# Who begins the wide weight loads and the rows of sums in an attention and feed-forward kernel: ScalarE's queue in place of SyncE's

## The chip, the cores and the metric

The kernel runs as one program on one core of a Trainium2 chip. A core has TensorE (PE), which multiplies matrices; VectorE (DVE), ScalarE (ACT) and GpSimd (POOL), which work element by element; SyncE (SP), which in this kernel only begins transfers; and 16 DMA engines that carry them out. The measure is the device time of one execution in microseconds (us); smaller is better.

## The reference, cut to what matters

```python
# attention: 4 batches, 8 heads, 576 rows, head size 64, causal by blocks of 64
scores = (1 / sqrt(D)) * q @ k.T
scores = where(block_i >= block_j, scores, -1e9)
attn = exp(scores - max(scores)); attn = attn / (sum(attn) + 1e-09)
x = (attn @ v) as [2304, 512]
# first feed-forward, 512 -> 1536 -> 512
xn = x / sqrt(mean(x * x) + 1e-06) * rms_g
g = xn @ w_gate;  x = (g * sigmoid(g) * (xn @ w_val)) @ w_out
# second feed-forward: 8 experts of 512 -> 1024 -> 512, weighted by P
P = exp(x @ gate - max), 8 times scaled by row sums and column sums
out = sum over e of P[:, e] * (relu(x @ w1[e]) @ w2[e])
```

All of it is in float32. A float32 operand is split into a high and a low part, and three fast products stand for one exact one.

## The kernel before, in words

**The planner.** The whole program is written down as a graph of operations. `G.op(engine, planned ns, function, r=, w=, prio=, lat=)` adds one: `r` and `w` are the buffers that it reads and writes, `lat` the planned time from its end to the start of what needs it, and `alts` other engines that may do it. `Graph.emit` then runs a list schedule forward and backward 24 times with these planned numbers, keeps the best, and writes the instructions out in that order. Each engine runs its own instructions strictly in that order. So a changed number or engine of one operation can move others, on every engine.

**The stages.** Attention takes the 32 heads one after another, four batches of eight. Heads 0 to 6 and 8 to 12 ("new" heads) make their scores twice: once for the maximum, once transposed for the exponent (L584, L587 on TensorE, L593 on ScalarE); their output and their sums of exponents come from one product (L620). The others normalise and transpose (L522, L683, L693, L733). The first feed-forward (L1007 up, L1066 down) works on five blocks of rows; its block 0 needs the first batch's attention, and it is laid between the heads of the next batches. The second feed-forward fills the rest.

**Rows of sums.** In `sv_d`, for each of the 12 new heads, the output of L620 is copied from PSUM to the buffer `tm` in two pieces, 512 and 64 wide (by ScalarE at L645, or by VectorE at L647, as the planner finds it better). Then a transfer of 2.2 KB spreads row 0, the sums, over 64 partitions (L653, begun by SyncE), VectorE adds 1e-9 and inverts (L657, L658), two more transfers write the result to DRAM and spread it over 64 partitions (L663, L664), and VectorE multiplies (L666, into `xx`).

**Wide loads.** The weights of the first feed-forward come as 64-bit words, 512 KB for a tile of 128 x 512. `convert` loads one into one of two buffers (L348, begun by SyncE; there are 36, 12 each of the matrices `wg`, `wv` and `wo`), ScalarE makes two integer parts (L350, L352), VectorE shifts (L354), GpSimd adds (L356, into `raw`). From `raw` come the high part (ACT, L294) and the low part (POOL or DVE, L307) of `w`, which SyncE stores for later blocks (L334) and reloads (L324). A wide load may begin when L350 and L352 of the load two before it are done.

**SyncE's queue** holds everything else too: q, k and v (L456, L457, L493, L494, L500), 1,093 transfers in all. It runs in order: a transfer that waits holds up those behind it. Eight semaphores are taken in turn by all transfers of the program, so a transfer also waits until the one that had its semaphore before has landed.

Of the kernel before, what the change touches and what calls it, by code (L numbers as in the profile page):

```python
# [12 lines left out]
U64 = mybir.dt.uint64  # L13
AF = mybir.ActivationFunctionType
# [183 lines left out]
def t_act(n, psum=False, ap=0):  # L198
    if ALONE:
        return (165 if psum else 190) + 0.845 * n + 144 * ap  # L200
    return (50 if psum else 92) + n / 1.2 + 90 * ap
# [9 lines left out]
def t_vv(n):  # L211
    return Both(150 + 1.04 * n if ALONE else t_v1(n))


def t_v1(n):
    return 150 + 1.04 * n if ALONE else 66 + n / 0.96


def t_v2(n):
    return Both(150 + n / 1.92 if ALONE else 120 + n / 0.96)  # L220


def t_pool(n):
    return Both(60 + 2.4 * n if ALONE else 60 + 2.28 * n)
# [11 lines left out]
def tile_attn_moe_moe2(ctx: ExitStack, tc: tile.TileContext, qT, kT, vP, wg, wv, wo, rg, gw, w1, w2, ident_d, mq_d, mk_d, bm_d, out):  # L236
    nc = tc.nc
# [11 lines left out]
    G = Graph()  # L249
# [10 lines left out]
    def fixed(t, par=False):  # L260
        return Buf(lambda: t, par=par)
# [50 lines left out]
    class Loader:  # L312
# [24 lines left out]
        def convert(self, src, raw, prio):  # L337

            wd, y, up = WIDE.next(), CVT[0].next(), CVT[1].next()

            def part(dt, i):
                return wd().bitcast(dt).rearrange("p (n w) -> p n w", w=2)[:, :, i]

            def i32(b):
                return b().bitcast(I32)

            ops = [
                G.op("SP", 2200, lambda: nc.sync.dma_start(out=wd().bitcast(U64), in_=src), w=[wd], prio=prio, lat=2000),  # L348

                G.op("ACT", t_act(512), lambda: nc.scalar.activation(out=y(), in_=part(F32, 1), func=AF.Prelu, scale=2.0**-112, alpha=2.0**32),  # L350
                     r=[wd], w=[y], prio=prio),
                G.op("ACT", t_act(512), lambda: nc.scalar.activation(out=i32(up), in_=part(U32, 0), func=AF.Copy, scale=2.0**-29),  # L352
                     r=[wd], w=[up], prio=prio),
                G.op("DVE", t_v2(512), lambda: nc.vector.tensor_scalar(  # L354
                    out=i32(y), in0=i32(y), scalar1=3, scalar2=None, op0=ALU.logical_shift_left), r=[y], w=[y], prio=prio),
                G.op("POOL", t_pool(512), lambda: nc.gpsimd.tensor_tensor(out=i32(raw), in0=i32(y), in1=i32(up), op=ALU.add),  # L356
                     r=[y, up], w=[raw], prio=prio),
            ]
            self.conv += ops
# [44 lines left out]
    def A(*a, **k):  # L404
        k.setdefault("prio", 1.0)
        o = G.op(*a, **k)
        att_ops.append(o)
        return o
# [209 lines left out]
    def sv(i, dst, d0, t, o, n, c, start, stop):  # L618
        p, vx = st["P", i][t], st["vs", i]
        A("PE", t_f32(n), lambda: nc.tensor.matmul(  # L620
            out=dst()[:, d0 : d0 + n], lhsT=vx()[:, c, :], rhs=p()[:, o : o + n], start=start, stop=stop),
            r=[vx, vones, p], w=[dst], prio=0.0)
# [13 lines left out]
    def sv_d(i):  # L636
        b, h = divmod(i, H)
        O, O2, r = st.pop(("O", i)), st.pop(("O2", i)), TM.next(par=True)
        sv(i, O2, 128, 0, 0, 64, 0, True, True)
        if h % 2 == 0:  # L640
            st["X", b, h // 2] = XX.next(par=True)
        X, p = st["X", b, h // 2], 64 * (h % 2)
        halves = ((O, 0, 64, 512), (O2, 128, 0, 64))
        for src, o, c, n in halves:
            A("ACT", t_act(n, True), lambda src=src, o=o, c=c, n=n: nc.scalar.activation(  # L645
                out=r()[:, c : c + n], in_=src()[:, o : o + n], func=AF.Copy), r=[src], w=[r],
              alts=[("DVE", t_v1(n), lambda src=src, o=o, c=c, n=n: nc.vector.tensor_copy(  # L647
                  out=r()[:, c : c + n], in_=src()[:, o : o + n]))], margin=0.0)
        sr, rc, rb, rd = SR.next(), RC.next(), (RB0 if i < H else RB1).next(), fixed(scr.tile([S], F32, name=f"rd{i}"))
        rt = lambda: O2()[0:64, 256 : 256 + S // 64]  # L650
        if i >= H:
            rb.before |= b0_ops
        A("SP", 600, lambda: nc.sync.dma_start(out=sr(), in_=r()[0:1, :].rearrange("o (p n) -> o p n", p=64)),  # L653
          r=[r], w=[sr], lat=2000, prio=0.5)

        def recip():
            nc.vector.tensor_scalar(out=rt(), in0=sr(), scalar1=1e-9, scalar2=None, op0=ALU.add)  # L657
            nc.vector.reciprocal(out=rc(), in_=rt())  # L658

        tmp = Buf(rt)  # L660
        tmp.before, tmp.users = O2.before, O2.users
        A("DVE", 380, recip, r=[sr], w=[rc, tmp], prio=0.5)
        A("SP", 600, lambda: nc.sync.dma_start(out=rd().rearrange("(p n) -> p n", p=64), in_=rc()), r=[rc], w=[rd], lat=2000, prio=0.5)  # L663
        A("SP", 600, lambda: nc.sync.dma_start(out=rb()[64:128], in_=rd().unsqueeze(0).to_broadcast([64, S])),  # L664
          r=[rd], w=[rb], lat=2000, prio=0.5)
        A("DVE", t_vv(S), lambda: nc.vector.tensor_tensor(  # L666
            out=X()[p : p + 64], in0=r()[64:128], in1=rb()[64:128], op=ALU.mult), r=[r, rb], w=[X])
# [261 lines left out]
    def attention():  # L929
# [8 lines left out]

        old = ((t_x0, nothing), (t_x1, pv_a), (t_x2, pv_b), (t_x3, pv_c), (nothing, pv_d))
        new = ((st_a, nothing), (st_b, sv_a), (st_c, sv_b), (st_d, sv_c), (nothing, sv_d))  # L940
        for i in range(NH + 1):
            p = i - 1
# [806 lines left out]
```

## Time and profile before

| | |
|---|---|
| time, median of 3 runs | 2167.6 us (2166.83 to 2169.93) |
| profiled execution, span from its first to its last instruction | 2165.9 us (no time of its own is listed beside it; the span is 1.7 us under the median) |
| busy share of the span | PE 99%, DVE 64%, POOL 53%, ACT 44% |
| granted TensorE clock, mean | 0.996 of full speed |
| DMA, mean | 194 GB/s |

Busy shares are means over stages that differ. TensorE's own share counts matrix products that overlap; where it waits, and for whom, is told by the waits and by the chain of work that ended last.

### The profile page before, as it was taken

The numbers are of one execution on the slowest core, as the hardware profiler recorded it, in microseconds if no ns is written. First come the engines' busy times: TensorE is split into PE (matmuls) and PEld (weight loads), VectorE is DVE, ScalarE is ACT, GpSimd is POOL, SyncE is SP. The second block draws the span as 40 slices with busy tenths as digits, with TensorE's granted clock in tenths as the row PEclk, the third lists the DMA queues.
The fourth block names the chain that finished last, engine by engine and source line by source line (L and its number), as shares of the span: only waits on it lengthen the run. The fifth ranks groups of instructions, "written<-read, shape, count | busy, mean of one in ns | idle before, by whom it ended". The sixth has DMA issues, their size and how long they took to land.

```text
span 2165.9 us, 31187 instructions
## 1 busy us (share of the span) xinstructions
PE 2136.3 (99%) x10964; PEld 1851.2 (85%) x10964; DVE 1376.3 (64%) x2366; ACT 954.7 (44%) x2074; POOL 1147.2 (53%) x1068
## 2 busy tenths in 40 slices
PE   8899999999999999999999999999999999999999
PEld 6677888888999999999999999999878888888887
DVE  7778776664633576555555555555777777777766
ACT  6669786762322433443433333333433333232332
POOL 6566534322423656565666566664556555464544
PEclk9999999999999999999999999999999999999999
DMA  6667875636766545445555555544655566556553
GB/s 181 212 178 238 272 227 187 199 121 195 244 229 218 199 176 176 175 176 190 179 185 182 187 191 183 187 175 171 223 190 198 200 192 222 188 202 203 195 195 117
DMA packets 164496, 419.88 MB, mean 194 GB/s; under 512 B 26138, under 2 KB 56026, under 8 KB 164340
## 3 DMA queue, kind: packets, MB, share of 16 engines
q1 hardware_dynamic: 164340, 417.90, 57.4%
q8 instruction: 86, 1.41, 0.3%
q14 instruction: 70, 0.57, 0.1%
HBM read 275.40 MB, written 141.09 MB: 192 GB/s over the span
## 4 chain that ended last, share of the span: by engine, by line
PE 92%; DVE 5%; ACT 2%; issue 1%; DMA 0%; SPq 0%; DVEq 0%; ACTq 0%
PE ps L1412 24%; PE pm L1480 20%; PE pm L1007 13%; PE pm L1637 11%; PE pm L1412 7%; PE pm L1066 6%; PE po L1637 3%; PE ps L506 2%; PE ps L693 1%; PE po L733 1%; PE po L620 1%; DVE mn L515 1%; ACT p L683 0%; PE po L1022 0%; DVE acc L354 0%
## 5 line engine op out<-in xcount | busy, mean ns | idle before, releaser
L1412 PE MATMUL ps<-xs,w 128*128 128x384 f32 (+2 forms) x2478 | 506.4, 346 | 2.4 <-DVE acc L1563 1.8
L1412 PEld LDWEIGHTS ps<-xs,w 128*128 128x128 f32 x2478 | 436.5, 188 | 48.9 <-DVE acc L1563 2.2
L1007 PE MATMUL pm<-x,w 128*128 128x512 f32 (+1 forms) x1440 | 346.5, 381 | 2.3 <-DVE t L1050 2.3
L1496 DVE SCALAR_TENSOR_TENSOR acc<-pm,Pm,acc 128x512 f32<-128x512 f32 x280 | 209.9, 750 | 182.0 <-PE pm L1480 182.0
L1007 PEld LDWEIGHTS pm<-x,w 128*128 128x128 f32 x1440 | 255.1, 190 | 31.2 <-DVE t L1050 2.4
L1480 PE MATMUL pm<-w,h 128*128 128x512 f32 x1152 | 280.0, 391 | 0.0
L307 POOL TENSOR_TENSOR w<-raw,w 128x512 fp32r<-128x512 f32 (+1 forms) x159 | 190.3, 1206 | 117.7 <-ACT w L294 104.4
L1480 PEld LDWEIGHTS pm<-w,h 128*128 128x128 f32 x1152 | 209.8, 188 | 39.4
L1480 PE MATMUL pm<-w,x 128*128 128x512 f32 x768 | 192.8, 393 | 0.0
L307 POOL TENSOR_TENSOR h<-t,h 128x512 fp32r<-128x512 f32 (+1 forms) x65 | 79.8, 1227 | 184.0 <-ACT h L294 171.4
L1480 PEld LDWEIGHTS pm<-w,x 128*128 128x128 f32 x768 | 142.5, 188 | 24.9
L1066 PE MATMUL pm<-h,w 128*128 128x512 f32 (+1 forms) x720 | 161.3, 372 | 0.0
L1618 DVE TENSOR_TENSOR acc<-pm,acc 128x512 f32<-128x512 f32 x169 | 116.1, 688 | 67.4 <-PE pm L1637 66.2
L1066 PEld LDWEIGHTS pm<-h,w 128*128 128x128 f32 x720 | 129.1, 188 | 15.8 <-DVE h L307 0.5
L1412 PE MATMUL pm<-xs,w 128*128 128x256 f32 (+2 forms) x654 | 138.5, 335 | 0.0
L1422 ACT ACTIVATE pad<-ps 128x256 f32<-128x256 f32 (+2 forms) x115 | 54.9, 477 | 181.0 <-PE ps L1412 180.6
L1637 PE MATMUL pm<-x,w 128*128 128x512 f32 x510 | 124.4, 389 | 0.0
L1412 PEld LDWEIGHTS pm<-xs,w 128*128 128x128 f32 x654 | 111.7, 188 | 14.5
L307 POOL TENSOR_TENSOR w<-pad,w 128x512 fp32r<-128x512 f32 x64 | 89.0, 1392 | 61.9 <-ACT w L294 61.5
L307 POOL TENSOR_TENSOR x<-pad,x 128x512 fp32r<-128x512 f32 (+1 forms) x67 | 93.6, 1400 | 50.2 <-ACT x L294 50.2
L1427 DVE TENSOR_TENSOR pad<-ps,pad 128x384 f32<-128x384 f32 (+2 forms) x127 | 66.1, 521 | 80.3 <-ACT pad L1422 46.8
L1422 ACT ACTIVATE t<-ps 128x384 f32<-128x384 f32 (+1 forms) x72 | 36.2, 503 | 180.4 <-PE ps L1412 180.4
(363 smaller groups left out, 4125.1 us busy)
## 6 DMA issues: line engine op xcount, KB each, us to landing
raw<-w_dram SPq DMA_DIRECT2D x128, 256.0 KB, 2.9
w<-kg SPq DMA_DIRECT2D x48, 512.0 KB, 4.3
w<-kv SPq DMA_DIRECT2D x48, 512.0 KB, 3.6
w<-ko SPq DMA_DIRECT2D x48, 512.0 KB, 3.8
fa<-w SPq DMA_DIRECT2D x32, 512.0 KB, 3.3
fd<-w SPq DMA_DIRECT2D x32, 512.0 KB, 3.9
fc<-w SPq DMA_DIRECT2D x32, 512.0 KB, 3.0
sb<-w SPq DMA_DIRECT2D x32, 512.0 KB, 4.7
```

The lines of the kernel that those rows point to most:

```text
L307: eng.tensor_tensor(out=out_(), in0=a(), in1=b(), op=ALU.subtract)
L506: nc.tensor.matmul(out=ps()[:, o : o + n], lhsT=a[:, 128 * t : 128 * t + 128], rhs=c[:, k0 : k0 + n], start=start, stop=stop)
L515: return A("DVE", t_v1(n), lambda: nc.vector.tensor_reduce(out=m()[:, col : col + 1], in_=ps()[:, o : o + n], axis=AX, op=ALU.max, negate= ...
L1007: nc.tensor.matmul(out=ps()[:, 0:n], lhsT=w()[:, a, 128 * k : 128 * k + 128], rhs=xv()[:, c, k, 0:n], start=k == 0 and (a, c) == (0, 0), s ...
L1066: nc.tensor.matmul(out=ps()[:, 0:n], lhsT=wos[q]()[:, a, 128 * m : 128 * m + 128], rhs=ht()[:, c, 0:n], start=q == 0 and (a, c) == (0, 0), ...
L1412: nc.tensor.matmul(out=bank()[:, 0:n], lhsT=w()[:, a, o + 128 * k : o + 128 * k + 128], rhs=views[p, q, i, k, c](), start=start and k == 0 ...
L1422: G.op("ACT", t_act(n, True), lambda: nc.scalar.activation(out=t()[:, 0:n], in_=bank()[:, 0:n], func=AF.Copy), r=[bank], w=[t])
L1427: G.op("DVE", t_v1(n), lambda: nc.vector.tensor_tensor(out=t()[:, 0:n], in0=bank()[:, 0:n], in1=t()[:, 0:n], op=ALU.add), r=[bank, t], w=[t])
L1480: nc.tensor.matmul(out=y(), lhsT=hs[f][half]()[:, a, o : o + 128], rhs=ws[f]()[:, c, :], start=f == 0 and (a, c) == (0, 0), stop=f == GF - ...
L1496: G.op("DVE", 63 + t_v1(512), lambda y=y, dst=dst, tt=tt, e=e: nc.vector.scalar_tensor_tensor(out=dst(), in0=wide(y()), scalar=Pm()[:, tt, ...
L1618: G.op("DVE", t_v1(N), lambda: nc.vector.tensor_tensor(out=dst(), in0=bank()[:, 0:N], in1=dst(), op=ALU.add), r=[bank, dst], w=[dst])
L1637: nc.tensor.matmul(out=bank()[:, 0:N], lhsT=w()[:, a, o : o + 128], rhs=ops[i][gi]()[:, c, 0:N], start=start and gi == 0 and (a, c) == (0, ...
```

## The change

Two kinds of transfer get another queue, with other planned numbers: the 36 wide loads (planned 2200 ns on SP and 2000 ns to landing, now 100 ns on ACT and 4200 ns) and the 12 rows of sums (600 and 2000 ns, now 100 and 2500 ns). The copies of the new heads' output lose VectorE as an alternative.

```diff
@@ convert
-G.op("SP", 2200, lambda: nc.sync.dma_start(out=wd().bitcast(U64), in_=src), w=[wd], prio=prio, lat=2000),
+G.op("ACT", 100, lambda: nc.scalar.dma_start(out=wd().bitcast(U64), in_=src), w=[wd], prio=prio, lat=4200),
@@ sv_d
     A("ACT", t_act(n, True), lambda src=src, o=o, c=c, n=n: nc.scalar.activation(
-        out=r()[:, c : c + n], in_=src()[:, o : o + n], func=AF.Copy), r=[src], w=[r],
-      alts=[("DVE", t_v1(n), lambda src=src, o=o, c=c, n=n: nc.vector.tensor_copy(
-          out=r()[:, c : c + n], in_=src()[:, o : o + n]))], margin=0.0)
+        out=r()[:, c : c + n], in_=src()[:, o : o + n], func=AF.Copy), r=[src], w=[r])
...
-A("SP", 600, lambda: nc.sync.dma_start(out=sr(), in_=r()[0:1, :].rearrange("o (p n) -> o p n", p=64)),
-  r=[r], w=[sr], lat=2000, prio=0.5)
+A("ACT", 100, lambda: nc.scalar.dma_start(out=sr(), in_=r()[0:1, :].rearrange("o (p n) -> o p n", p=64)),
+  r=[r], w=[sr], lat=2500, prio=0.5)
```

Lines of the changed kernel from 646 on carry a number smaller by two (L653 is L651 there). The planner's order changes on every engine in the first part. Of TensorE's 10,769 matrix instructions the last 9,059 stand in the same order as before; in the profile of before they begin between 360 and 400 us. The number of matrix instructions is unchanged, ScalarE has 48 transfers more and SyncE 48 fewer, and the five copies that VectorE did at L647 (one 512 wide, four 64 wide) are ScalarE's.

ScalarE at the very start of the program. In these rows `acc` with a number is scratch room in the accumulators (`acc_63` the two wide buffers, `acc_64` their integer parts, `acc_61` loaded q and k), `ka`, `qa`, `kb`, `qb` and `x` the split operands of the scores, `rq` loaded q, k or mask rows, and DMAHW0 to DMAHW7 the eight semaphores of transfers. Before:

```order
L294 ACT_TABLE_LOAD [waits DMAHW1_49]
L294 ACTIVATE ka_106<-acc_61 128x576 [waits DMAHW0_49]
L294 ACTIVATE qa_102<-rq_112 128x576 [waits DMAHW3_49,DMAHW2_49]
L294 ACTIVATE qb_104<-rq_112 64x576
L294 ACTIVATE qb_104<-rq_110 64x576 [waits DMAHW5_49,DMAHW4_49,DVE_49]
L294 ACTIVATE qb_105<-rq_110 64x576
L294 ACTIVATE x_84<-rq_110 64x576
L294 ACTIVATE kb_109<-rq_111 64x576 [waits DMAHW7_49,DMAHW6_49,DVE_49]
L294 ACTIVATE x_85<-rq_110 64x576
L294 ACTIVATE kb_108<-rq_111 64x576
```

and in the changed kernel:

```order
L348 DMA acc_63<-wg_dram 128x512
L348 DMA acc_63<-wv_dram 128x512
L294 ACT_TABLE_LOAD [waits DMAHW2_49]
L294 ACTIVATE ka_106<-acc_61 128x576 [waits DMAHW1_49]
L350 ACTIVATE acc_64<-acc_63 128x512 [waits DMAHW0_49]
L294 ACTIVATE qa_102<-rq_112 128x576 [waits DMAHW5_49,DMAHW4_49]
L294 ACTIVATE qb_104<-rq_112 64x576
L294 ACTIVATE qb_104<-rq_110 64x576 [waits DMAHW7_49,DMAHW6_49,DVE_49]
L294 ACTIVATE qb_105<-rq_110 64x576
L294 ACTIVATE kb_109<-rq_111 64x576 [waits DMAHW1_49,DMAHW0_49,DVE_49]
L294 ACTIVATE x_84<-rq_110 64x576
L294 ACTIVATE x_85<-rq_110 64x576
```

Two wide loads now stand ahead of everything on ScalarE (before, the first of them was begun at 26.44 us), and the first conversion step L350 stands between the first two splits.

The sixth wide load, the second of `wo`. Before, it stands in SyncE's queue (`rd` is the inverted sums in DRAM, `rv` loaded v, `rgs` the norm's weights):

```order
L935 DMA rgs<-rg_dram 128x4 [waits DMAHW1_49]
L653 DMA acc_62<-tm_146 64x1x9 [waits DMAHW2_49,Activation_49]
L664 DMA x_85<-rd_150 64x576 [waits DMAHW5_49,DMAHW3_49]
L500 DMA rv_114<-vP_dram 128x320 [waits DMAHW4_49]
L456 DMA rq_112<-qT_dram 64x576
L457 DMA rq_112<-qT_dram 64x576 [waits DMAHW6_49]
L348 DMA acc_63<-wo_dram 128x512 [waits DMAHW7_49]
```

and in the changed kernel in ScalarE's (`p` are exponents, `po`, `pm` and `ps` PSUM banks, `vs` a split v, `mn` maxima):

```order
L593 ACTIVATE p_0_117<-pm_92 128x64 [waits PE_49]
L294 ACTIVATE x_84<-acc_65 128x576 [waits DMAHW7_49]
L294 ACTIVATE x_84<-acc_65 128x576 [waits DMAHW2_49,DMAHW0_49]
L350 ACTIVATE acc_64<-acc_63 128x512 [waits DMAHW1_49]
L348 DMA acc_63<-wo_dram 128x512 [waits DMAHW5_49,Activation_49]
L294 ACTIVATE vs_116<-rv_114 128x5x64 [waits DMAHW4_49]
L645 ACTIVATE tm_146<-po_96 128x512 [waits PE_49]
L645 ACTIVATE tm_146<-pm_92 128x64 [waits PE_49]
L571 ACTIVATE acc_62<-mn_132 128x5 [waits DVE_49]
L651 DMA acc_62<-tm_146 64x1x9 [waits DMAHW3_49,Activation_49]
L352 ACTIVATE acc_64<-acc_63 128x512 [waits Pool_49]
```

It no longer stands behind the transfers of sums, v and q on SyncE, but ScalarE's rows now stand behind the waits of two transfers. The L350 that uses this load stands 15 rows behind it. Of the 48 transfers on ScalarE 36 wait for one of the eight semaphores.

## Rows read from the trace of the kernel before

**Rows 1.** The page: span, and the chain that ended last by engine.

```profile
span 2165.9 us, 31187 instructions
PE 92%; DVE 5%; ACT 2%; issue 1%; DMA 0%; SPq 0%; DVEq 0%; ACTq 0%
```

**Rows 2.** Stretches: PE, PEld, DVE, ACT, POOL busy us (x); clock, DMA share, GB/s.

```profile
0.00:60.00 60.00, 53.79 (x256) 38.41 (x256) 43.14 (x105) 42.56 (x96) 39.69 (x53) 1.00 0.64 180
60.00:80.00 20.00, 15.02 (x65) 10.77 (x65) 14.78 (x35) 16.88 (x41) 9.29 (x8) 0.83 0.55 183
...
90.00:130.00 40.00, 33.50 (x149) 26.23 (x147) 28.45 (x57) 23.90 (x53) 22.31 (x22) 0.91 0.51 167
...
150.00:200.00 50.00, 49.68 (x259) 39.85 (x258) 43.86 (x87) 46.17 (x117) 32.74 (x28) 1.00 0.76 239
200.00:240.00 40.00, 37.24 (x190) 29.61 (x189) 36.35 (x75) 32.64 (x76) 27.92 (x22) 1.00 0.79 245
...
360.00:1400.00 1040.00, 1039.55 (x5772) 945.03 (x5771) 575.71 (x1069) 421.80 (x958) 531.45 (x548) 1.00 0.54 189
```

**Rows 3.** Waits of TensorE, whole span: us in total, times, longest.

```profile
PE po L620 <- ACT p L593: 2.3, 1, 2.3
PE pm L1007 <- DVE t L1050: 2.3, 1, 2.3
...
PE pm L693 <- ACT p L683: 1.8, 1, 1.8
```

**Rows 4.** The chain, 53 to 65 us: start us, us, what ran.

```profile
53.91 1.28 SPq L664
...
57.02 6.09 DMA acc<-wo_dram
...
64.26 0.58 ACT p L593
```

**Rows 5.** ScalarE in order of time: start us, us, what [idle before <-ended by].

```profile
49.62 0.70 ACT L352 ACTIVATE acc<-acc 128x512 int32<-128x512 uint32 x1
...
63.14 0.67 ACT L350 ACTIVATE acc<-acc 128x512 f32<-128x512 f32 x1 [1.97 <-DMA acc<-wo_dram]
```

**Rows 6.** Stretches in which the granted clock was at half, columns as in rows 2.

```profile
64.67:68.09 3.42, 3.20 (x4) 1.51 (x5) 1.47 (x3) 3.42 (x12) 1.81 (x2) 0.50 0.83 322
...
74.91:78.33 3.42, 3.42 (x12) 2.48 (x12) 2.90 (x7) 3.21 (x9) 1.27 (x1) 0.50 0.66 169
98.81:102.22 3.41, 3.41 (x10) 2.63 (x9) 3.41 (x8) 2.53 (x6) 1.94 (x2) 0.50 0.61 115
```

**Rows 7.** Line L348: issue ns min/median/max, first and last; who waited (us, times).

```profile
L348 SPq DMA_DIRECT2D acc<-wg_dram x12: 333/478/1548, 26.4 to 286.0; - x12
L348 SPq DMA_DIRECT2D acc<-wv_dram x12: 333/380/577, 33.3 to 293.6; - x12
L348 SPq DMA_DIRECT2D acc<-wo_dram x12: 328/358/584, 47.7 to 309.7; - x12
...
  ACT acc L350: 7.8, 6
```

**Rows 8.** Line L653, the rows of sums: issue ns min/median/max.

```profile
L653 SPq DMA_DIRECT2D acc<-tm x12: 481/498/1500, 23.3 to 168.6; - x12
```

**Rows 9.** The page's DMA issues: KB each, median us to landing.

```profile
acc<-wg_dram SPq DMA_DIRECT2D x12, 512.0 KB, 4.2
```

**Rows 10.** The start in order of time: start us, us, what.

```profile
4.16 0.29 SPq L429 DMA_DIRECT2D rq<-mk_dram  x1
...
5.71 0.68 ACT L294 ACTIVATE ka<-acc 128x576 fp32r<-128x576 f32 x1
...
6.29 0.67 ACT L294 ACTIVATE qa<-rq 128x576 fp32r<-128x576 f32 x1
...
11.14 0.47 PE L506 MATMUL ps<-kb,qb 96*128 96x448 f32 x1
```

**Rows 11.** The first 10 us as a stretch, columns as in rows 2.

```profile
0.00:10.00 10.00, 5.78 (x7) 2.52 (x8) 6.66 (x21) 5.57 (x9) 5.14 (x21) 1.00 0.50 139
```

## The prediction, made before the changed kernel was run

> **What bounds the kernel now.** I read the page first: the chain of work that ended last is TensorE for 92% of the span, and SyncE's queue has 0% of it [rows 1]. So time can only be won where TensorE stands still or runs at half clock. The table of stretches says where that is: from 360 us on TensorE is busy without a break, 1039.55 of 1040 us in the longest stretch, and its order there is the same in the changed kernel; in 60:80 it is busy for 15.02 of 20 us, in 90:130 for 33.50 of 40, in 200:240 for 37.24 of 40 [rows 2]. The change acts in just that part, since the last wide load is begun at 309.7 us [rows 7].
>
> The longest waits of TensorE in the kernel's body are one each of 2.3 us for an exponent (L593), 2.3 us for L1050 and 1.8 us for L683 [rows 3]. The chain of waits tells what stands behind the first: SyncE is at L664 until 55.19, comes after three more transfers to the wide load of `wo` at 57.02, and 6.09 us later it has landed; the exponent starts at 64.26 [rows 4]. ScalarE in order of time shows the link. L352 of the load two before ended at 49.62 + 0.70 = 50.32 us, so the buffer was free 6.7 us before SyncE came to the load. ScalarE reached L350 early and stood for 1.97 us until 63.14, and the exponents that TensorE needed were queued behind it [rows 5]. The pauses cost a second time: after each, the granted clock is at half (1.2 instead of 2.4 GHz) for 3.4 us [rows 6].
>
> **What is removed.** The sixth wide load goes to ScalarE's queue, 15 rows ahead of the L350 that needs it. If it is begun when its buffer is free, that stall goes: 2.3 us of TensorE's wait and half of the 3.4 us at half clock, 1.7 us, together 4.0. The wait of 1.8 us for L683 at 73 us, with its own 1.7 us of half clock, may go too, since ScalarE was late there by the 2 us that it had stood: 7.5 us at most. At least it is 0, when ScalarE is late for another reason (below). I take 4.0: the first wait has the load as its only cause, the second not. The other waits of L350 for wide loads, 7.8 us in 6 [rows 7] with this one, are waits of ScalarE that TensorE did not show. SyncE is relieved of 12 x (0.478 + 0.380 + 0.358) + 12 x 0.498 = 20.6 us of issues [rows 7, 8]. I price that at nothing beyond the stall: in the chain SyncE has 0% [rows 1].
>
> **What is added on ScalarE.** No row of before shows a transfer begun there. Each of the 48 costs at least nothing (the queue issues it while the instruction ahead still runs) and at most what SyncE takes, 0.36 to 0.50 us [rows 7, 8]. What of it reaches TensorE depends on the cover. In 0:60 and 90:130 ScalarE is idle for 17 and 16 us [rows 2] and can hide the issues there. In 60:80 it is busy 16.88 of 20 us, in 150:200 46.17 of 50 [rows 2]; there is no cover. By the changed order, set beside the products that ran in those stretches before, 12 of the 48 fall into them. At 0.5 us that is 6.0 us of ScalarE; nothing at the least. I take half, 3.0, because in 150:200 VectorE is nearly as full (43.86 of 50) and ScalarE is not always the later one. The five copies that come from VectorE are outweighed: in exchange the planner gives VectorE five of ScalarE's copies of `qb`.
>
> **What moves at the start.** Two wide loads are now begun before anything else on ScalarE, which stood idle there until the first k had landed. L350 comes between `ka` (5.71 us) and `qa` (6.29 us), and TensorE's first full pair of products at 11.14 us ends a chain of such copies [rows 10], which follow each other every 0.57 us: +0.57. And SyncE's rows now share the semaphores: the mask rows that it began at 4.16 us [rows 10] take the semaphore of the first wide load, which, begun at about 0.7 and landing in 4.2 us [rows 9], is back at about 4.9: +0.8. Nothing covers either, since TensorE has no other work yet: +1.3 together. At least 0.6 (the landing is no later than the copies' turn); at most 3.0, when 1 MB beside q and k, on DMA engines that are half busy [rows 11], delays the second load's semaphore as well.
>
> At one place a rule can be set against the trace. The rows say that SyncE's issues have no share of the chain except in one stretch around 55 us [rows 1, 4]. The Trainium skill, "DMA: Bandwidth & Descriptors", section "Issuing engines are not separate DMA queues", says that transfers begun by different engines run on the same 16 DMA engines, and that beginning them from several saves only issue time, usually small beside the transfer. By that rule the first term would be 0, and the sum 2165.9 + 1.3 + 3.0. The trace agrees but for that one stretch, where a load went out 6.7 us late.
>
> **The sum**, against the profiled execution's span: 2165.9 - 4.0 + 3.0 + 1.3 = 2166.2 us. The median of the runs is 1.7 us above that span, so I predict 2168 us. That is no change: about 0.2%, 4.3 us, is what a measurement of this kernel can tell.
>
> **The rivals.**
>
> *Faster: all waits behind late loads go.* Both waits in 60:80 vanish (-7.5). With weights converted earlier the next blocks' products are ready when TensorE runs dry in 90:130, so the wait of 2.3 us for L1050 and its half-clock stretch (98.81 to 102.22, 1.7 us) go too: -4.0. Issues on ScalarE are hidden (0), the start costs 1.3. That gives 2167.6 - 7.5 - 4.0 + 1.3 = 2157 us. For it: SyncE's queue runs behind the free buffers, and the changed order begins loads earlier. Against it: at 98 us TensorE waits behind the norm's chain on VectorE, not for weights, and in 60:80 ScalarE has no room. Chance of ending more than 0.2% faster: 0.33.
>
> *Slower: ScalarE is held at its issues.* A transfer waits until the one eight before it has landed, mostly one of SyncE's, and 36 of the 48 issues do so. On SyncE only other transfers stood behind such a wait; on ScalarE the exponents (L593, L522), the copies out of PSUM (L645) and the splits for the next head stand there, and TensorE waits for all of them. Priced at one place of SyncE's queue, 0.5 us, for each of the 12 issues without cover, it is 6.0, on top of the full 6.0 for the issues themselves and 1.3 at the start, with nothing gained in 60:80 since ScalarE stays late there: 2167.6 + 13.3 = 2181 us. It decides when more than about 0.35 us an issue is lost at the 12 places (4.0 gained over 12). For it: SyncE ran up to 6.7 us behind. Against it: relieved of 48 issues it runs less behind. Chance of ending more than 0.2% slower: 0.30. [...]
>
> *It does nothing.* The loads are hidden anyway, and the issues cost nothing: 2167.6 + 1.3 = 2169 us. For it stands SyncE's 0% of the chain. Chance 0.15; the forecast itself has 0.22.
>
> **How the numbers follow.** Forecast and last rival end within 0.2%: 0.37 together; faster 0.33; slower 0.30. The likeliest case alone reaches from 2163 to 2172. The range must hold 8 in 10, so it takes in the faster case to 2156, just beyond its 2157, and the slower one to 2180, and leaves some 0.1 beyond each end for an order that fits better or worse than any row shows.
>
> **What would show it.** Stall removed: no wait of L350 for `wo` near 60 us, TensorE busy for over 17 of the 20 us before the first L1007, one half-clock stretch fewer. Issues: transfers among ScalarE's rows with their durations; under 0.1 us of lost time at each would refute my 3.0, over 0.5 confirm the slower rival, and so would waits of ScalarE put down to SyncE's transfers. Start: the first product with `kb` later than 11.14 us by about 1.3. What would make me wrong most: a stretch that is now free of waits, 240 to 360 us, which becomes short of operands because the new order lays attention closer together, or a pause more that halves the clock for another 3.4 us.

## The result, and the profile of the changed kernel

The changed kernel takes 2195.4 us (median of 4 runs, 2193.96 to 2200.97) against 2167.8 us before: a ratio of 1.0125, 95% interval 1.0113 to 1.0137, or 27.1 us more. The prediction was 2168 us with a range of 2156 to 2180. It was wrong.

The page of the changed kernel, its span and its chain, to be set beside [rows 1]:

```profile
span 2193.4 us, 31178 instructions
PE 89%; DVE 3%; DMA 2%; ACT 1%; issue 1%; POOL 0%; SPq 0%; ACTq 0%; DVEq 0%
```

Transfers, 0% of the chain before, now have 2% of it. The stretches of the changed kernel, columns as in [rows 2]:

```profile
0.00:60.00 60.00, 44.31 (x163) 31.77 (x164) 35.52 (x83) 32.71 (x70) 30.14 (x43) 0.80 0.69 195
60.00:80.00 20.00, 17.82 (x96) 13.61 (x94) 16.02 (x33) 13.61 (x33) 10.79 (x12) 0.99 0.58 173
80.00:90.00 10.00, 9.31 (x26) 6.46 (x26) 2.81 (x9) 6.81 (x22) 4.79 (x4) 0.50 0.69 176
90.00:130.00 40.00, 34.41 (x155) 26.84 (x154) 30.36 (x69) 24.38 (x49) 20.43 (x18) 0.87 0.43 148
...
150.00:200.00 50.00, 44.06 (x205) 34.62 (x204) 35.01 (x67) 34.55 (x79) 27.55 (x27) 0.93 0.72 222
...
240.00:360.00 120.00, 115.56 (x622) 96.67 (x622) 96.80 (x209) 92.98 (x241) 46.74 (x44) 0.99 0.64 201
360.00:1400.00 1040.00, 1039.83 (x5754) 943.98 (x5753) 574.37 (x1080) 426.72 (x965) 530.41 (x542) 1.00 0.55 189
```

From 360 us on TensorE is as busy as before, as predicted. The first 60 us are worst: 44.31 us of TensorE at a mean clock of 0.80, where before there were 53.79 at 1.00 [rows 2]. In 60:80, where the gain was expected, TensorE is busier (17.82 against 15.02), though the work that falls into it is no longer the same. Over the first 360 us, in four stretches of each kernel (before first), the sums are:

```profile
sum 360.00, PE 338.53 PEld 270.12 DVE 274.30 ACT 274.52 POOL 207.13; mean PE 84.63 PEld 67.53 DVE 68.58 ACT 68.63 POOL 51.78
sum 360.00, PE 323.03 PEld 256.69 DVE 264.46 ACT 256.12 POOL 179.87; mean PE 80.76 PEld 64.17 DVE 66.11 ACT 64.03 POOL 44.97
```

So TensorE stands 15.5 us longer. The other 12 us or so are put down to work at half clock, by subtraction alone. The stretches of the changed kernel at half clock, to be set beside [rows 6]:

```profile
14.83:28.48 13.65, 11.78 (x38) 9.88 (x39) 10.15 (x22) 8.45 (x19) 8.90 (x8) 0.50 0.69 194
48.96:59.20 10.24, 8.65 (x26) 6.33 (x26) 6.19 (x14) 5.32 (x14) 5.53 (x7) 0.50 0.61 188
79.68:89.92 10.24, 9.23 (x24) 6.40 (x25) 2.81 (x9) 7.13 (x23) 5.11 (x5) 0.50 0.70 182
...
sum 54.60, PE 47.17 PEld 36.20 DVE 33.16 ACT 33.28 POOL 29.79; mean PE 6.74 PEld 5.17 DVE 4.74 ACT 4.75 POOL 4.26
```

54.6 us at half clock ahead of 360 us, in seven stretches; before there were four, of 3.4 us each. How long the clock is at half does not tell the loss by itself: e9 below has 27.3 us of it and takes 0.7 us more than the kernel before, and e8 has 27.3 us too and takes 11.9 us more. TensorE stands 28.9 us of the first 360 in e8 and 19.7 in e9 (21.5 before). TensorE's waits in the whole span:

```profile
PE ps L506 <- DVE acc L656: 4.4, 3, 3.1
...
PE ps L691 <- ACT p L522: 3.9, 2, 2.9
PE pm L584 <- POOL qa L307: 3.8, 1, 3.8
PE pm L506 <- DVE acc L656: 3.2, 2, 2.6
...
PE pm L1005 <- DVE t L1048: 2.3, 1, 2.3
```

The wait for L593 of 2.3 us that headed [rows 3] is down to 0.5. L1005 is the old L1007 and keeps its 2.3 us. New is L656, 7.6 us in 5: it is VectorE's inversion of a row of sums, whose intermediate result lies in a PSUM bank that the next score product needs. ScalarE's exponents of the heads that are not new (L522) follow with 5.8 us in 3, and one wait of 3.8 us for `qa` (L307) stands at the start.

How the start went, engines together, in order of time:

```profile
0.73 0.39 ACTq L348 DMA_DIRECT2D acc<-wg_dram  x1
...
1.15 0.45 ACTq L348 DMA_DIRECT2D acc<-wv_dram  x1
...
5.54 0.25 SPq L429 DMA_DIRECT2D rq<-mk_dram  x1
...
8.44 0.48 SPq L456 DMA_DIRECT2D acc<-qT_dram  x1
8.50 1.28 ACT L294 ACT_TABLE_LOAD   x1 [8.50 <-DMA acc<-kT_dram]
...
9.79 0.68 ACT L294 ACTIVATE ka<-acc 128x576 fp32r<-128x576 f32 x1
...
10.38 0.66 ACT L350 ACTIVATE acc<-acc 128x512 f32<-128x512 f32 x1
...
13.56 0.50 PE L584 MATMUL pm<-qa,ka 128*128 128x512 f32 x1 [3.78 <-POOL qa L307]
...
15.79 0.74 PE L506 MATMUL ps<-kb,qb 96*128 96x448 f32 x1 [1.53 <-ACT kb L294]
```

The first k has landed at 8.50 us, so `ka` begins at 9.79 and not 5.71 [rows 10]; SyncE begins the mask rows at 5.54 (4.16 before) and the next q at 8.44. From 2.5 to 8.0 us the DMA engines are busy for 0.99 of the time (0.63 before). TensorE stands 3.78 us until 13.56 and 1.53 us more until the first product with `kb` at 15.79, which is 4.65 us later than before; the clock is at half for 13.65 us from 14.83 on.

Further on, the chain from 141 to 156 us shows what a new wait for L656 consists of:

```profile
141.30 1.96 DMA rd<-acc
143.26 6.11 DMA kv<-w
...
149.39 0.02 ACTq L651
...
149.44 6.11 DMA acc<-tm
...
155.58 0.17 DVE ps L655
...
155.78 0.22 DVE acc L656
...
156.04 1.27 PE ps L506 x4
```

ScalarE's row of sums (L651, the old L653) may go only when a store of converted weights (`kv`) that SyncE began at 143.26 has landed. Its 2.2 KB then take 6.11 us; a wide load begun at 147.50 and k, q and v begun from 147.61 on are under way beside it, and which of them holds it up is not shown. The inversion waits for it, and TensorE for the inversion, 3.10 us; the clock is at half from 154.77 to 161.60.

### The profile page after: what moved, and what is told of

Read it like the earlier page. It is cut to its first block, busy times and chain, and to the rows that moved or that the text cites. A ratio compares the mean times of both kernels' runs of the same rounds, so it can differ in the third digit from the quotient of the medians.

```text
span 2193.4 us, 31178 instructions
## 1 busy us (share of the span) xinstructions
PE 2149.2 (98%) x10964; PEld 1862.2 (85%) x10964; DVE 1382.5 (63%) x2376; ACT 950.5 (43%) x2071; POOL 1137.1 (52%) x1061
## 4 chain that ended last, share of the span: by engine, by line
PE 89%; DVE 3%; DMA 2%; ACT 1%; issue 1%; POOL 0%; SPq 0%; ACTq 0%; DVEq 0%
PE ps L1410 24%; PE pm L1478 20%; PE pm L1005 12%; PE pm L1635 11%; PE pm L1410 7%; PE pm L1064 6%; PE po L1635 3%; PE ps L506 1%; PE ps L691 1%; PE po L731 1%; DMA acc<-tm 0%; PE po L1020 0%; DMA acc<-wv_dram 0%; ACT p L522 0%; DVE xs L307 0%
## 5 line engine op out<-in xcount | busy, mean ns | idle before, releaser
L1005 PE MATMUL pm<-x,w 128*128 128x512 f32 (+1 forms) x1440 | 344.7, 380 | 2.3 <-DVE t L1048 2.3
L1005 PEld LDWEIGHTS pm<-x,w 128*128 128x128 f32 x1440 | 256.1, 191 | 31.4 <-DVE t L1048 2.4
L307 POOL TENSOR_TENSOR w<-raw,w 128x512 fp32r<-128x512 f32 (+1 forms) x158 | 188.4, 1201 | 115.7 <-ACT w L294 112.4
L307 POOL TENSOR_TENSOR h<-t,h 128x512 fp32r<-128x512 f32 (+1 forms) x63 | 76.9, 1221 | 179.3 <-ACT h L294 171.3
L307 POOL TENSOR_TENSOR w<-pad,w 128x512 fp32r<-128x512 f32 x64 | 89.0, 1392 | 61.8 <-ACT w L294 61.3
L307 POOL TENSOR_TENSOR x<-pad,x 128x512 fp32r<-128x512 f32 (+1 forms) x67 | 94.2, 1411 | 45.1 <-ACT x L294 44.8
```

The costliest lines, as they stand in the source:

```text
L307: eng.tensor_tensor(out=out_(), in0=a(), in1=b(), op=ALU.subtract)
L1005: nc.tensor.matmul(out=ps()[:, 0:n], lhsT=w()[:, a, 128 * k : 128 * k + 128], rhs=xv()[:, c, k, 0:n], start=k == 0 and (a, c) == (0, 0), s ...
```

## The experiments

All ratios are to runs of the kernel before on the same chip; a difference in us is (ratio - 1) x 2168. The diffs show of each line only what matters; dots stand for the rest.

| run | us | ratio (95%) | us more |
|---|---|---|---|
| e1 changed order, SyncE issues | 2196.6 | 1.0132 (1.0115 to 1.0149) | 28.6 |
| e2 old order, ScalarE issues | 2166.6 | 0.9989 (0.9980 to 0.9999) | -2.4 |
| e3 wide loads only | 2199.2 | 1.0142 (1.0126 to 1.0157) | 30.8 |
| e4 rows and copies only | 2174.0 | 1.0026 (1.0016 to 1.0035) | 5.6 |
| e6 first loads held | 2186.0 | 1.0076 (1.0061 to 1.0091) | 16.5 |
| e8 planned numbers only | 2182.6 | 1.0055 (1.0040 to 1.0070) | 11.9 |
| e9 2300 ns | 2170.2 | 1.0003 (0.9994 to 1.0013) | 0.7 |
| e10 rows planned late | 2195.8 | 1.0123 (1.0106 to 1.0140) | 26.7 |
| e14 two loads early | 2175.1 | 1.0029 (1.0018 to 1.0040) | 6.3 |
| e11 held and paced | 2190.7 | 1.0093 (1.0078 to 1.0108) | 20.2 |
| e12 3300 ns | 2185.3 | 1.0078 (1.0061 to 1.0095) | 16.9 |
| e13 copies only | 2173.9 | 1.0025 (1.0016 to 1.0035) | 5.4 |
| c1 rows 700 ns | 2174.2 | 1.0024 (1.0014 to 1.0034) | 5.2 |
| c2 landing 2100 ns | 2171.6 | 1.0018 (1.0009 to 1.0027) | 3.9 |
| c3 changed, landing 4300 ns | 2194.7 | 1.0120 (1.0105 to 1.0135) | 26.0 |
| c4 1100 ns | 2170.8 | 1.0003 (0.9993 to 1.0012) | 0.7 |
| g1 changed, 2200 ns kept | 2175.0 | 1.0030 (1.0020 to 1.0039) | 6.5 |
| g2 600 ns | 2173.8 | 1.0028 (1.0017 to 1.0039) | 6.1 |

### The order or the queue: e1 and e2

The planner decides the order from the numbers and the engine's name; the function that it is given decides which queue issues. So the two can be crossed. e1, the changed kernel with

```diff
-G.op("ACT", 100, lambda: nc.scalar.dma_start(out=wd()...), ..., lat=4200)
+G.op("ACT", 100, lambda: nc.sync.dma_start(out=wd()...), ..., lat=4200)
-A("ACT", 100, lambda: nc.scalar.dma_start(out=sr()...), ..., lat=2500, prio=0.5)
+A("ACT", 100, lambda: nc.sync.dma_start(out=sr()...), ..., lat=2500, prio=0.5)
```

> The changed kernel's order on every engine, but SyncE begins the 48 transfers, each at the place in its queue that the order gives. Theory P (the plan: with wide loads priced at 100 ns the order starts two of them at once and leads on to an order that the transfers cannot keep): the loss stays, 2188 to 2205 us, first product with kb again after 15 us. Theory Q (the queue: ScalarE's issues, or transfers of two queues in each other's way): most of the 27 us goes, 2166 to 2176 us.

e2, the kernel before with

```diff
-G.op("SP", 2200, lambda: nc.sync.dma_start(out=wd()...), ..., lat=2000)
+G.op("SP", 2200, lambda: nc.scalar.dma_start(out=wd()...), ..., lat=2000)
-A("SP", 600, lambda: nc.sync.dma_start(out=sr()...), ..., lat=2000, prio=0.5)
+A("SP", 600, lambda: nc.scalar.dma_start(out=sr()...), ..., lat=2000, prio=0.5)
```

> The order of the kernel before on every engine (copies with VectorE as alternative too), but ScalarE begins the 48 transfers, each at the place in ScalarE's stream that the old order gives. Theory P: no change, 2163 to 2172 us. Theory Q: 2180 to 2200 us, with waits of TensorE for L593 or L657 that the kernel before does not have.

The order carries the loss whole: 28.6 us with SyncE issuing, and -2.4 us when ScalarE issues the same 48 transfers in the old order. Theory Q falls. The start in e1 is milder than expected there, the first product with `kb` coming at 14.25 us and not after 15, and the loss is the same. e1 shows the new waits too:

```profile
PE ps L506 <- DVE acc L656: 13.1, 4, 5.2
PE pm L506 <- DVE acc L656: 4.2, 3, 1.7
```

They grow to 17.3 us, and so they are no matter of ScalarE's queue. What an issue costs ScalarE is read from e2, ScalarE in order of time at 61 us, in the stretch where the prediction saw no cover:

```profile
61.33 0.50 ACTq L653 DMA_DIRECT2D acc<-tm  x1
61.88 0.66 ACT L350 ACTIVATE acc<-acc 128x512 f32<-128x512 f32 x1 [0.93 <-DMA acc<-wo_dram]
62.45 0.66 ACT L352 ACTIVATE acc<-acc 128x512 int32<-128x512 uint32 x1
63.01 0.57 ACT L593 ACTIVATE p<-ps 128x512 f32<-128x512 f32 x1
63.04 0.34 ACTq L348 DMA_DIRECT2D acc<-wg_dram  x1
63.49 1.24 ACT L593 ACTIVATE p<-pm 128x512 f32<-128x512 f32 x4
```

The wide load at 63.04 is issued in 0.34 us while the exponent of 63.01 still runs, and the next exponent follows at once, with no idle time in brackets. The row at 61.33 is issued where ScalarE is idle, and there it had to wait for `wo` anyway. TensorE in e2 at the place where it had waited 2.3 us for L593:

```profile
62.15 0.50 PE L587 MATMUL ps<-x 128*128 128x512 f32 x1 [2.00 <-DVE x L578]
```

It still stands for 2.00 us, now for VectorE, and the clock is at half for 3.41 us from 63.48 on.

### Which part of the change: e3, e4, e13, e8

e3 is the kernel before with the change's line in `convert` alone; e4 has its edits in `sv_d` alone (rows of sums and copies).

```diff
e3
-G.op("SP", 2200, lambda: nc.sync.dma_start(out=wd()...), ..., lat=2000)
+G.op("ACT", 100, lambda: nc.scalar.dma_start(out=wd()...), ..., lat=4200)
e4
-      alts=[("DVE", t_v1(n), ...)], margin=0.0)
-A("SP", 600, lambda: nc.sync.dma_start(out=sr()...), ..., lat=2000, prio=0.5)
+A("ACT", 100, lambda: nc.scalar.dma_start(out=sr()...), ..., lat=2500, prio=0.5)
```

> Only the 36 wide loads as in the change (queue and planned numbers); rows of sums and copies as before. If the early start and the dense wide loads carry the loss (theory P): 2185 to 2198 us. If the loss is the rows of sums that stand right behind a wide load in one queue (theory R: landings of 4.5 to 6 us in place of 2 to 3): rows leave that queue, 2172 to 2182 us, and VectorE waits under 2 us for them.

> Only the 12 rows of sums and their copies as in the change; wide loads as before. Theory P: 2163 to 2172 us. Theory R: no wide load is ahead of the rows in ScalarE's queue, so also 2163 to 2172 us; ScalarE's issue alone as cause: 12 times 0.5 us and a clock pause, 2175 us or more.

The wide loads' line alone gives 30.8 us, with 12.3 us of waits for the inversion though the rows are SyncE's again; the edits in `sv_d` alone give 5.6. e13 is the kernel before with only the copies' alternative taken away:

```diff
-      alts=[("DVE", t_v1(n), ...)], margin=0.0)
```

> The kernel before, only that the copies of the new heads' output have lost VectorE as alternative; wide loads and rows of sums as before. Rows of sums and copies together gave 2174.0. If the copies carry that: 2172 to 2177 us. If the rows' queue and numbers do: 2165 to 2170 us.

It gives 5.4 us. The copies account for e4, whose 2174.0 us lie above what P and R gave; the rows' queue and numbers add nothing that can be told from zero. e8 leaves every queue alone and changes two numbers of the kernel before:

```diff
-G.op("SP", 2200, lambda: nc.sync.dma_start(out=wd()...), ..., lat=2000)
+G.op("SP", 100, lambda: nc.sync.dma_start(out=wd()...), ..., lat=4200)
```

> The kernel before, only with the wide loads' planned numbers changed on SyncE (100 ns and 4200 ns to landing in place of 2200 and 2000); no queue changes. Theory S: SyncE still begins q and k first, so no loss at the start: 2166 to 2176 us. Theory D: the plan no longer keeps 2.2 us of SyncE for each load, rows of sums and q, k land late: 2182 to 2200 us.

11.9 us, with every transfer on the queue of before. In e8 the wide loads stand behind the first q and k in SyncE's queue, and the start is as before:

```profile
10.93 0.47 PE L506 MATMUL ps<-kb,qb 96*128 96x448 f32 x1 [0.67 <-ACT kb L294]
```

So these 11.9 us come from later places. The 18.9 us between e8 and e3 come with planning the loads on ScalarE, which is free at the start: in e3 the first product with `kb` comes at 15.52 us. e14 below prices that start at 6.3 us; where the rest of the 18.9 us is lost was not separated.

### The start: e6 and e14

e6 is the changed kernel with the wide loads, and so the first two, planned only after the q and k of heads 0 and 1 have landed (`first_loads` are these and the other transfers that the graph holds up to there):

```diff
-G.op("ACT", 100, ..., w=[wd], prio=prio, lat=4200)
+G.op("ACT", 100, ..., w=[wd], prio=prio, lat=4200, after=first_loads)
```

> The changed kernel, but the first two wide loads are allowed only after the loads of heads 0 and 1 have landed; all else is planned anew with the changed numbers. Theory S (the two loads at the start, which delay k, q and SyncE's queue, and the pauses with half clock after them, carry the loss): the first product with kb is back at about 11 us and the extra 15 us lost before 60 us go, 2176 to 2184 us. Theory D (wide loads that follow too densely everywhere, so that q, k and rows of sums land later than planned): at most 5 us of it, 2188 to 2198 us.

The first product with `kb` is back at 11.62 us, and of the 27.1 us 16.5 stay. That lies 2 us above the range of theory S and 2 us below that of theory D: the start is a part, not the whole. e6 plans everything anew, so its size is not clean. e14 keeps the old order word for word and only begins the first two wide loads ahead of all else, from ScalarE; their conversion stays in place:

```diff
-best = end, [o.fn for o in order]
+best = end, [o.fn for o in sorted(order, key=lambda o: o not in self.early)]
...
-G.op("SP", 2200, lambda: nc.sync.dma_start(out=wd()...), ..., lat=2000)
+G.op("SP", 2200, lambda: wide_load(out=wd()...), ..., lat=2000)
```

> The kernel before in its own order, with one difference: the first two wide loads are begun by ScalarE ahead of everything, as in the change; their conversion stays where it was. Theory S (1 MB ahead of k and q is the price of the start): first product with kb at 14 to 16 us in place of 11.1, and with a clock pause 2172 to 2180 us. My price in the prediction, 1.3 us: 2168 to 2171 us.

Its start, ScalarE and then TensorE (lines there are numbered 7 higher):

```profile
8.59 1.28 ACT L294 ACT_TABLE_LOAD   x1 [8.59 <-DMA acc<-kT_dram]
9.89 0.68 ACT L294 ACTIVATE ka<-acc 128x576 fp32r<-128x576 f32 x1
10.47 0.67 ACT L294 ACTIVATE qa<-rq 128x576 fp32r<-128x576 f32 x1
...
15.32 0.74 PE L513 MATMUL ps<-kb,qb 96*128 96x448 f32 x1 [0.47 <-ACT kb L294]
```

k lands at 8.59 (4.4 before) without any other change, with the DMA engines again 0.99 busy from 2.5 to 8.0 us, and the time is 6.3 us longer. Without L350 between `ka` and `qa` the product comes 0.47 us sooner than in the changed kernel, about what the prediction gave that place (0.57).

### Late rows of sums: e10

The changed kernel, with the plan told that a row takes long:

```diff
-A("ACT", 100, ..., r=[r], w=[sr], lat=2500, prio=0.5)
+A("ACT", 100, ..., r=[r], w=[sr], lat=5000, prio=0.5)
```

> The changed kernel, but the rows of sums are planned with 5000 ns to landing in place of 2500, about what the trace shows where one stands behind a wide load. Theory R (late rows hold VectorE, the inversion, and so the PSUM bank that TensorE needs): TensorE's waits for L656, 7.6 us in 5, go, with their clock pauses 8 to 14 us: 2181 to 2188 us. Theory S: the start is as before this edit, 2190 to 2198 us.

TensorE's waits in e10:

```profile
PE pm L1005 <- DVE t L1048: 4.3, 1, 4.3
...
PE ps L506 <- DVE acc L656: 0.6, 1, 0.6
```

The waits for the inversion are down from 7.6 us to 0.6, and the time is the same, 26.7 us more. Theory R falls as the cause: the late rows are where TensorE stood, and with them out of the way it stands elsewhere.

### How much time is kept for a load, and what any other order costs: e9, e11, e12, c1 to c4, g1, g2

e11 is e6 with the wide loads planned on a queue of their own, "WQ", that no other transfer uses; ScalarE issues them.

```diff
-G.op("ACT", 100, ..., lat=4200, after=first_loads)
+G.op("WQ", 2200, ..., lat=2000, after=first_loads)
```

> The changed kernel with the first two wide loads held until heads 0 and 1 are loaded, as in the run before, and with the wide loads planned on a queue of their own that each occupies for 2200 ns (2000 ns to landing); ScalarE begins them. Theory D, by spacing (wide loads planned too close to each other): 2168 to 2177 us. Theory O, by shared occupancy (the 2200 ns counted because they stood on the same planned queue as q, k, v and the rows of sums): no better than 2180 us.

20.2 us: spacing the loads among themselves does not help, theory D by spacing falls, and theory O's range is met. The others change planned numbers alone (e9: SyncE's planned ns for a wide load; e12, c4, g2: these ns and the landing; c1: the row's 600; c2 and c3: the landing), but for g1, the changed kernel with the load's planned queue and numbers of before:

```diff
e9   -("SP", 2200, ..., lat=2000)    +("SP", 2300, ..., lat=2000)
e12  -("SP", 2200, ..., lat=2000)    +("SP", 3300, ..., lat=1000)
c4   -("SP", 2200, ..., lat=2000)    +("SP", 1100, ..., lat=3100)
g2   -("SP", 2200, ..., lat=2000)    +("SP", 600, ..., lat=3600)
c1   -("SP", 600, ..., lat=2000)     +("SP", 700, ..., lat=2000)
c2   -("SP", 2200, ..., lat=2000)    +("SP", 2200, ..., lat=2100)
c3   -("ACT", 100, ..., lat=4200)    +("ACT", 100, ..., lat=4300)
g1   -("ACT", 100, nc.scalar, lat=4200)   +("SP", 2200, nc.scalar, lat=2000)
```

> A control: the kernel before with 2300 ns planned for a wide load in place of 2200, a number without meaning that gives another order. Theories S and D: near the kernel before, 2162 to 2175 us. Theory L (any other order costs this, since the kernel before is the lucky one of many): 2180 us or more.

> The kernel before with 3300 ns of SyncE planned for a wide load and 1000 ns to landing (2200 and 2000 before, the sum nearly the same). Theories D and O, by the dose: no loss, 2160 to 2172 us, since 100 ns gave 2182.6, 2200 gave 2167.8, 2300 gave 2170.2. If 2200 is a point that the rest is tuned to: 2174 us or more.

> The kernel before with 700 ns planned for a row of sums in place of 600, a change without meaning. Theory L (spread of orders: nearly any other order costs some us): 2172 to 2185 us. Theory N (the numbers' meaning): 2164 to 2171 us.

> The kernel before with 2100 ns to the landing of a wide load in place of 2000, a change without meaning. Theory L: 2172 to 2185 us. Theory N: 2164 to 2171 us.

> The changed kernel with 4300 ns to the landing of a wide load in place of 4200, a change without meaning. Theory L: anywhere from 2178 to 2200 us. Theory N: the two loads still start first and nothing reserves time for them, so 2190 to 2199 us.

> The kernel before with 1100 ns of SyncE planned for a wide load and 3100 ns to landing (2200 and 2000 before, the sum the same). Theory N: between the two ends measured, 2172 to 2178 us. Theory L: no relation to the dose, anything from 2166 to 2188 us.

> The changed kernel (ScalarE begins all 48 transfers, copies on ScalarE alone), only that the plan keeps 2200 ns of SyncE for a wide load and 2000 ns to landing, as before. Theory N (the planned time of the wide loads carries all but the spread): 2168 to 2177 us. If ScalarE's queue costs something with this order after all: 2180 us or more.

> The kernel before with 600 ns of SyncE planned for a wide load and 3600 ns to landing. Theory N, a loss that grows as the planned time falls below what a load takes: between 2170.8 (1100 ns) and 2182.6 (100 ns), 2172 to 2180 us. Theory L: 2166 to 2172 us as often as not.

Three numbers without meaning (e9, c1, c2) cost 0.7, 5.2 and 3.9 us: another order around the kernel before costs up to some 5 us by itself (theory L, in that size). The copies' 5.4 us lie about at that bound and are not told apart from it. Around the changed kernel such a number (c3) moves nothing beyond the interval. By planned time the loss goes 11.9 us at 100 ns, 6.1 at 600, 0.7 at 1100, 0 at 2200, 0.7 at 2300: only the 100 ns lie clearly outside the spread, with 600 at its edge (theory N). e12, 16.9 us at 3300 ns with a landing of 1000, contradicts the rule "more time kept, no loss"; a planned time far off on either side costs. In e12 SyncE stands 59.6 us ahead of 360 us at wide loads whose buffer ScalarE has not freed (37.4 before); that this is its cause was not shown. g1 is the decisive one for the change: with ScalarE issuing all 48 transfers and only the loads' planned queue and numbers put back, the loss is 6.5 us, so the planned queue and numbers together carry 27.1 - 6.5 = 20.6 us. The numbers are not enough: e11 has the same 2200 and 2000 ns on a queue of its own and loses 20.2 us. It differs from g1 in that queue and in the hold on the first loads, and in e6 that hold came with a gain. So the 2200 ns seem to help where they take room on the planned queue of q, k and v (theory O); no run changes that alone.

No run beats the kernel before clearly; e2, at -2.4 us with an interval that ends just under 1, is the best of them.

## Why the prediction was wrong, point by point

**What bounds the kernel** held: all of the difference lies ahead of 360 us, in 15.5 us more of TensorE's pauses and in stretches at half clock.

**What is removed**, 4.0 us: the late load was there, and the price does not come out. e2 has a part of this term without the new order: the load of `wo` goes out at 55.80 us, 1.2 us sooner than before, and ScalarE stands 0.93 us at L350 in place of 1.97 [rows 5]. But TensorE stands at that place for 2.00 us in place of 2.3, for VectorE's L578, and half clock follows as before. So "the load as its only cause" is not borne out: with the load sooner, VectorE is late there. e2 is 2.4 us faster in all; what the whole term is worth alone, no run shows. The list of TensorE's longest waits in the prediction leaves one out that is longer than the 1.8 us for L683: 1.9 us for L578 at 117 us. The Trainium skill, "DMA: Bandwidth & Descriptors", section "Issuing engines are not separate DMA queues", says that transfers begun by several engines run on the same 16 DMA engines, and that this saves only the time of beginning them, which is usually small; e2's 2.4 us for 48 transfers agree.

**What is added on ScalarE**, +3.0 us: too high. The issues slip under the instruction that runs. They take ScalarE 0.334 us for a wide load and 0.479 for a row in e2 (medians), no longer than SyncE's 0.36 to 0.50. e2 is below zero in all, so even if the whole 4.0 us had been gained there, at most 1.6 us would be left for them.

**What moves at the start**, +1.3 us, at most 3.0: mis-sized. It is 6.3 us in e14. The prediction counted one semaphore's turn and one copy, and took the landing of 4.2 us as given. What happened is that the 1 MB filled the DMA engines beside k and q: k landed at 8.5 us in place of 4.4, and a long stretch at half clock followed the pause. The upper end named the case, "1 MB beside q and k", and priced it too low, from engines that were "half busy" [rows 11]. That 0.50 is a mean over the first 10 us; from 2.0 to 4.4 us, while k was on its way, they were 0.76 busy.

**What the sum had no term for** is the step that failed most: the order. The prediction went through three places of it and took the rest as equal in worth, with "some 0.1 beyond each end for an order that fits better or worse". In the changed kernel the wide loads' planned queue and numbers carry 20.6 us (g1), of which the start is some 6, if what e14 measured in the old order holds in the new one. With 100 ns for a load of 512 KB the plan keeps no time for it on any queue. The new order is shown to cost 11.9 us even on SyncE with a good start (e8). The pauses come from several places (late rows at L656, ScalarE's exponents at L522, q at the start at L307), and clearing one (e10) brings out others.

**The signs.** No wait of L350 for `wo` stands near 60 us in the changed kernel, as foretold for a stall that is removed; the half-clock stretch fewer did not come, there are three more. The kernel did show what the prediction named as likely to make it wrong most: 240 to 360 us is no longer free of waits (115.56 us busy against 119.63), and there is not one pause more that halves the clock but several.

**The rivals.** "Slower: ScalarE is held at its issues" had the sign and not the cause: e1 and e2 together refute it. A transfer that waits for another's semaphore does hold up a row of sums at 149 us in the chain above, but e1 has the same loss without ScalarE's queue. Of "Faster" only the busier TensorE in 60:80 came.

**Open** is which transfers or conversions of the cheap plan make up the 12 us of e8, why 3300 ns (e12) are no better, and whether it is SyncE's planned queue alone that parts g1 from e11. Late rows alone and spacing alone are excluded.

## What to carry to other kernels

Where a planner writes the order, a planned number is part of the program: cross the two (the new order with the old queue, the old order with the new queue) before crediting a queue with anything. A transfer that is planned as nearly free goes to the front wherever an engine stands idle, and its bytes then run beside the first operands that everything waits for. And measure what a meaningless change of a number costs, here up to 5 us, before a smaller effect is explained.

## What the runs showed of the hardware that was not expected

Two loads of 512 KB begun at 0.73 and 1.15 us put off the landing of k (two transfers of 144 KB, begun at 0.73 and 1.40) from 4.4 to 8.5 us. Pauses of 3.78 and 1.53 us came with 13.65 us at half clock, in which TensorE was busy for 11.78; before, no such stretch was longer than 3.42. And 48 issues on ScalarE, in the old order, cost nothing that can be measured.
